# Batch 0 of an attention and MLP kernel begun in groups of 256 tokens, with q and k loaded by token

## The chip, the cores and the metric

The kernel runs on one core of a Trainium2 chip. A core has five engines that work side by side, each through its own list of instructions in strict order: TensorE (PE, matrix products; its weight loads are shown as PEld), VectorE (DVE), ScalarE (ACT), GpSimd (POOL) and SyncE (SP). DMA transfers can be issued by SP, ACT and POOL; those of SP and ACT are called hardware loads here, those of POOL software loads. The metric is device time in microseconds of one execution; the profile is of one execution.

## The reference

Attention over 4 batches of 8 heads, 768 tokens and head dimension 64, with a window of 128 tokens and 4 sink tokens that everyone sees, then a two-layer MLP with a squared relu on the 3072 rows that result:

```
scores = scale * np.matmul(q, k.transpose(0, 1, 3, 2))
keep = is_sink | in_window
scores = np.where(keep, scores, -1000000000.0)
a = np.exp(scores - max); a = a / (sum(a) + 1e-09)
x = np.matmul(a, v)            # heads side by side: 3072 x 512
g = np.maximum(x @ w_in, 0.0) ** 2     # 512 x 2048
out = g @ w_out                        # 2048 x 512
```

All inputs and the output are float32.

## The kernel before, in words

The batches are handled one after the other, overlapped. Within a batch the tokens are taken in blocks of 256 (three blocks, called s = 0, 1, 2 in the code) and the heads in four pairs (m = 0 to 3). For a pair and a block the steps are: q and k turned, so that the head dimension lies on the partitions (transposes on PE into a PSUM tile `pt`, then an "unload" that copies `pt` to `qkT`); scores on PE into `ps`; exponential on ACT into `expm`; a mask (DVE or POOL; in block 0 of batch 0 the mask is added by two matmuls of `sg`, so no mask step follows); values on PE into `po`; the division by the sum ("norm", a reciprocal and a product on DVE) into `xn_sb`; four transposes on PE into `px` and a copy to `xT`. Then layer 1 (`pm`, 16 matmuls for 4 of 16 column blocks and one block of tokens), relu (`r`), square (`gT_sb`) and layer 2 (`py`). For the sinks, `kblk` is filled by ACT from `qkT`, `pk` is a PE product with it, `es` its exponential on ACT, and `vs` a product on POOL that reads `vs_in`, a small load of the sink rows of v.

Batch 0 has the start to itself. Before the change its first two blocks come as one group of 512 tokens: eight loads of 256 KB, for k and q of each pair in turn, all issued by SP (line 351). Four tokens lie side by side on a partition, so each piece of memory read is 1 KB long. They arrive as fp32 in `qr`. A cast regroups them to bf16 (`qs`, line 194 on DVE, line 192 on ACT), PE turns four 128 x 128 tiles per load (line 507), and the unload puts tokens back in their order with a strided write. The third block comes later, loaded and cast by POOL (`qn`). Weights (`w_in_sb`, `w_out_sb`) and v are loaded and cast by POOL too.

What sets the order of all work is a list written out by hand in the file: `ORDER` names every step by its number, with a letter for the engine where there is a choice (`d` DVE, `a` ACT) and the PSUM pool behind a plus. The steps are recorded in that order, and each engine gets its instructions in it. `DUMMIES` gives, for some steps, a number of filler matmuls (line 185) that PE runs ahead of the step while it would otherwise wait. Line 1368 is a run of 29 such matmuls at the start. A hardware load signals its end on one of eight semaphores used in turn; a load that takes a semaphore again first waits for the load that had it before.

## Time and profile before

| | |
|---|---|
| median of three runs | 210.17 us (209.14 to 210.32) |
| span of the profiled execution | 208.6 us |
| what lies around the span, against the median | 1.6 us |
| PE busy in the span | 199.8 us, 96% |
| DVE, ACT, POOL busy | 86%, 64%, 47% |
| first layer-1 product on PE | at 17.13 us |

The profiled execution's own time is given as its span; the runs are timed without a profile. A row of the profile in order of time reads: start, length (both us), engine, line, operation, output and inputs, count, and in brackets how long the engine had been idle and what ended that. "PE 96%" is not a peak: fillers and waiting pipelines count as busy.

### The profile page before, as it was taken

To read this page: it belongs to the slowest core of one execution; us is meant where nothing else is said; L and a number is where in the kernel's file an instruction comes from. 1 tells how busy PE (TensorE), PEld (TensorE's weight loads), DVE (VectorE), ACT (ScalarE), POOL (GpSimd) and SP (SyncE) were. 2 spreads that over 40 slices of the span, in tenths; PEclk is the share of its full clock that TensorE was granted. 3 is DMA by queue.
4 is the path that set the end of the run, shared out by engine and by line. 5 is a ranking of instruction groups with operands and counts; after the bars stand their busy time and mean duration, and the time that the engine had idled before them with its cause. 6 is when DMAs were issued, how large, how long until landed. Compare 5 with 4: busy or idle time off the path is not lost.

```text
span 208.6 us, 6015 instructions
## 1 busy us (share of the span) xinstructions
PE 199.8 (96%) x2498; PEld 176.1 (84%) x2500; DVE 178.4 (86%) x342; ACT 133.0 (64%) x208; POOL 98.2 (47%) x138
## 2 busy tenths in 40 slices
PE   7789899999899999999999999999999999999993
PEld 7548796679778889989878988998889999999893
DVE  5757566996989998999998788999989998998853
ACT  2595728548988168899888448989871452584110
POOL 7988164999489936999423628000280000000000
PEclk9999999999999999999999999999999999999999
DMA  5999999999989999999998996901023220200205
GB/s 150 280 185 204 178 193 214 170 155 188 121 55 135 146 142 210 126 167 155 140 149 216 95 129 172 155 3 25 3 50 123 57 80 24 104 0 0 100 4 201
DMA packets 93994, 26.10 MB, mean 125 GB/s; under 512 B 86800, under 2 KB 91408, under 8 KB 93968
## 3 DMA queue, kind: packets, MB, share of 16 engines
q0 software_dynamic: 69248, 12.59, 79.6%
q1 hardware_dynamic: 24536, 13.01, 27.0%
q8 instruction: 19, 0.31, 0.6%
q10 hardware_dynamic: 184, 0.14, 0.2%
q14 instruction: 7, 0.06, 0.1%
HBM read 27.30 MB, written 6.29 MB: 161 GB/s over the span
## 4 chain that ended last, share of the span: by engine, by line
PE 65%; POOL 12%; DVE 9%; DMA 6%; ACT 3%; issue 2%; POOLq 0%; ACTq 0%
PE py L1238 25%; PE pm L891 25%; DMA w_in_sb<-in_moe_w_in_dram 6%; PE pm L763 4%; PE ps L613 4%; POOL v L381 3%; PE po L682 3%; POOL qn L372 3%; POOL vs L554 2%; PE py L1099 2%; ACT expm L634 1%; POOL expm L218 1%; PE pt L507 1%; DVE sg L1212 1%; POOL w_in_sb L308 1%
## 5 line engine op out<-in xcount | busy, mean ns | idle before, releaser
L634 ACT ACTIVATE expm<-ps 128x1024 bf16<-128x1024 f32 (+1 forms) x48 | 43.9, 951 | 9.4 <-PE ps L613 7.5
L218 POOL TENSOR_SCALAR_AFFINE_SELECT expm<-expm 128x512 bf16<-128x512 bf16 x34 | 25.4, 782 | 43.8 <-DVE xn_sb L699 19.5
L941 DVE CUSTOM_DVE_ANT_0 r<-pm,t 128x512 bf16<-128x512 f32 x54 | 36.1, 685 | 1.6 <-PE pm L891 1.1
L1238 PEld LDWEIGHTS <-gT_sb 128*128 128x128 bf16 x320 | 30.4, 98 | 4.5 <-issue 0.8
L891 PEld LDWEIGHTS <-w_in_sb 128*128 128x128 bf16 x384 | 32.4, 114 | 1.7 <-issue 1.5
L192 ACT ACTIVATE t<-pm 128x512 f32<-128x512 f32 x42 | 24.7, 600 | 13.5 <-PE pm L891 12.7
L891 PEld LDWEIGHTS <-wi 128*128 128x128 bf16 x288 | 24.7, 114 | 0.8 <-issue 0.7
L1238 PEld LDWEIGHTS <-sg 128*128 128x128 bf16 x240 | 22.4, 98 | 3.2 <-DVE sg L1212 0.3
L192 ACT ACTIVATE osb<-py 128x256 f32<-128x256 f32 (+1 forms) x36 | 14.1, 398 | 15.7 <-PE py L1238 15.0
L763 PE MATMUL pm<-xT,w_in_sb 128*128 128x256 bf16 x192 | 22.5, 273 | 1.0 <-DMA w_in_sb<-in_moe_w_in_dram 1.0
L763 PEld LDWEIGHTS <-w_in_sb 128*128 128x128 bf16 x192 | 20.5, 114 | 1.9 <-DMA w_in_sb<-in_moe_w_in_dram 1.2
L891 PE MATMUL pm<-xs,wi 128*128 128x256 bf16 (+1 forms) x192 | 21.6, 246 | 0.0
L891 PE MATMUL pm<-xs,w_in_sb 128*128 128x256 bf16 (+1 forms) x192 | 21.5, 246 | 0.0
L1238 PE MATMUL py<-wt,gT_sb 128*128 128x256 bf16 x160 | 20.7, 273 | 0.2
L1238 PE MATMUL py<-wt,sg 128*128 128x256 bf16 x160 | 20.8, 273 | 0.0
L1238 PE MATMUL py<-w_out_sb,gT_sb 128*128 128x256 bf16 x160 | 20.4, 273 | 0.0
L914 ACT ACTIVATE gT_sb<-r 128x1024 bf16<-128x1024 bf16 x17 | 18.0, 1056 | 1.8 <-DVE r L941 1.6
L682 PE MATMUL po<-v,expm 128*128 128x65 bf16 x352 | 17.9, 193 | 0.3 <-ACT expm L634 0.3
L682 PEld LDWEIGHTS <-expm 128*128 128x128 bf16 x352 | 16.7, 97 | 1.7 <-ACT expm L634 0.5
L699 DVE TENSOR_TENSOR xn_sb<-po,rc 128x512 bf16<-128x512 f32 (+1 forms) x28 | 17.2, 615 | 1.0
L1252 DVE TENSOR_TENSOR osb<-py,osb 128x256 f32<-128x256 f32 x30 | 12.1, 418 | 4.7 <-PE py L1238 4.6
L613 PE MATMUL ps<-qkT 64*128 64x128 bf16 (+1 forms) x256 | 14.3, 238 | 0.8 <-ACT expm L634 0.6
(109 smaller groups left out, 383.3 us busy)
## 6 DMA issues: line engine op xcount, KB each, us to landing
out_dram<-osb SPq DMA_DIRECT2D x11, 512.0 KB, 4.9
v<-in_v_dram POOLq DMA_DIRECT2D x24, 128.0 KB, 6.8
qn<-in_k_dram POOLq DMA_DIRECT2D x20, 128.0 KB, 6.5
qn<-in_q_dram POOLq DMA_DIRECT2D x20, 128.0 KB, 6.4
w_in_sb<-in_moe_w_in_dram POOLq DMA_DIRECT2D x4, 512.0 KB, 10.5
w_out_sb<-in_moe_w_out_dram POOLq DMA_DIRECT2D x4, 512.0 KB, 10.9
qr<-in_k_dram SPq DMA_DIRECT2D x4, 256.0 KB, 5.6
qr<-in_q_dram SPq DMA_DIRECT2D x4, 256.0 KB, 5.2
```

The costliest lines, as they stand in the source:

```text
L192: return nc.scalar.activation(out=dst, in_=src, func=AF.Copy)
L218: nc.gpsimd.affine_select(out=e_tile, in_=e_tile, compare_op=ALU.is_ge, fill=fill, base=i - 1, pattern=[[0, n], [1 if i else -1, 128]], ch ...
L613: nc.tensor.matmul(ps[:, h2, o:o + w], lhsT=qkT_sb[r, m, 1, c, :], rhs=qkT_sb[r, m, 0, qb:qb + w // 128, :], start=(i == 0 and not biased) ...
L634: nc.scalar.activation(out=x[:, :, o:512], in_=bank_t["s", b, s, m][:, :, o:512], func=AF.Exp, scale=scale)
L682: touch(("po", b, s, m0), e, nc.tensor.matmul(pv[:, i, h2, :], lhsT=lhsT, rhs=rhs, start=(n_ == 0), stop=(n_ == len(mms) - 1)), j)
L699: touch(("po", b, s, m0), e, nc.vector.tensor_tensor(out=xn_sb[:, 2 * s:2 * s + 2, 128 * (m0 + j0):128 * (m0 + j0 + nj)].rearrange("p i (j ...
L763: nc.tensor.matmul(pm[:, i, :], lhsT=w_in_sb[:, fb // 4, kb, fb % 4:512:4], rhs=xT[:, c0 // 256:(c0 + cw) // 256, kb, :], start=(kb == 0), ...
L891: touch(tag, e, nc.tensor.matmul(y[:, bk, i, :], lhsT=weights(name, f0 + i, a), rhs=rhs[:, a, :], start=fresh and i == 0 and a == 0, stop= ...
L914: nc.scalar.activation(out=d, in_=x, func=AF.Square)
L941: touch(tag, e, nc.vector._custom_dve(TENSOR_ADD_SAT, out=d.rearrange("p n c -> p (n c)"), in0=T["y"][:, 1].rearrange("p n c -> p (n c)"), ...
L1238: touch((b, u), e, nc.tensor.matmul(region(name), lhsT=x[:, i, :], rhs=w_[:, i, :], start=first and i == 0, stop=i == HB - 1, skip_group_c ...
L1252: ins = nc.vector.tensor_tensor(out=d, in0=region(of), in1=d, op=ALU.add)
```

## The change

- Batch 0 now comes in three groups of 256 tokens. The first two are loaded by 16 transfers of 128 KB, each for 128 tokens and four heads, one token per partition, so that each piece read is 256 bytes long. k is issued by SP, q by ACT, ahead of the small `vs_in` load that ACT issued first before.
- The casts are gone. PE turns the fp32 tiles themselves, against an fp32 copy of the identity (`ident32`, made by one DVE copy), eight tiles for two head pairs at a time, into fp32 PSUM. The unload casts to bf16 and writes without a stride.
- The first 180 or so steps of `ORDER` stand in another order, and the fillers in `DUMMIES` are placed anew (31 behind the start before, 46 now). From the third block of batch 0 on the list is the old one with new numbers.

```diff
 ORDER = """
-986 0 1 2 7 8 9 10 11 12 13 14 15 16 17 18 987+0 3 5 19 20 21 6 79 22 23 24 25 55d 56d 57+0 58 59 60a 83+0 85 103+1
...
+975 0 1 8 9 10 11 12 13 14 15 16 17 18 19 976+0 3 7 5 20 21 22 6 4 23 24 25 62 2 56+0 57d 58a 64+1 66 65+1 59+0 67 60d
...
 DUMMIES = {
-    987: 29, 58: 8, 63: 10, 64: 4, 83: 3, 91: 3, 97: 3,
+    976: 29, 59: 8, 72: 6, 85: 6, 76: 4, 88: 6, 80: 4, 103: 6, 145: 6,
 }
...
     def fill_one(i):
+        nc.vector.memset(v_sb[i][:, :, :, D:D + 1], 1.0)
         nc.vector.memset(kblk[i], 0.0)
         nc.vector.memset(vs_sb[i], 0.0)
-        nc.vector.memset(v_sb[i][:, :, :, D:D + 1], 1.0)
...
+    def build_ident32(e):
+        nc.vector.tensor_copy(out=ident32, in_=ident)
...
-    GROUPS[0] = [(0, 4), (512, 2)]
+    GROUPS[0] = [(0, 2), (256, 2), (512, 2)]
...
+    def load_qk(g, half, ti):
+        if not half:
+            qr_slot[ti, g] = Slot("qr", 2)
+        h0 = NP * half
         def run(e):
+            if not half:
+                qr_t[ti, g] = bank(qr_slot[ti, g], "qr", [128, 2, DM], FP32)
+            return [(nc.scalar, nc.sync)[ti].dma_start(
+                out=qr_t[ti, g][:, t, D * h0:D * h0 + D * NP].rearrange("p (h d) -> p h d", d=D),
+                in_=(q, k)[ti][0, h0:h0 + NP, 256 * g + 128 * t:256 * g + 128 * t + 128, :].rearrange("h p d -> p h d"))
+                for t in range(2)]
+        o = dma_op(("act", "sp")[ti], ("qk", 0, half, ti, g), run, 1.0, None, () if half else [qr_slot[ti, g]])
...
-                    def regroup(e, m=m, ti=ti):
-                        t = qs_t[b, m, ti, g] = bank(qs_slot[b, m, ti, g], "qs", [128, w, n, 2, D], BF16)
-                            copy(e, t[:, 0], qr_t[b, m, ti, g].rearrange("p h (t d) -> p t h d", d=D))
...
-                            bank_t[b, m, g] = bank(bs, "pt", [128, 2, 1024], BF16)
+                            bank_t[b, m, g] = bank(bs, "pt", [128, 2, 1024] if casted else [128, 2, 512],
+                                                   BF16 if casted else FP32)
...
-                                        if casted else qs[ti][:, j, t, :, :], rhs=ident, is_transpose=True,
+                                        if casted else qr_t[ti, g][:, t, 128 * (m + j):128 * (m + j) + 128],
+                                        rhs=ident if casted else ident32, is_transpose=True,
...
-    load_sinks("act", 0)
-    for m in range(NP):
-        for ti in (1, 0):
-            load_qk(0, m, ti, 0, 1)
+    for g in range(2):
+        for half in range(2):
+            for ti in (1, 0):
+                load_qk(g, half, ti)
+    load_sinks("act", 0)
```

ACT's list at the start, before, with the semaphores that each instruction waits for (DMAHW0 to DMAHW7 are those of hardware loads; `qkT<-pt` is an unload, `expm<-ps` an exponential, `qs<-qr` a cast):

```order
L424 DMA vs_in<-in_v_dram 32x1x64
L192 ACT_TABLE_LOAD
L192 ACTIVATE qkT_179<-pt 128x512 [waits PE_49]
L634 ACTIVATE expm<-ps 128x2x384 [waits PE_49]
L634 ACTIVATE expm<-ps 128x1024 [waits PE_49]
L192 ACTIVATE qkT_179<-pt 128x512 [waits PE_49] x2
L192 ACTIVATE qs<-qr 128x512 [waits DMAHW7_49,DVE_49]
L192 ACTIVATE qs<-qr 128x512 [waits DMAHW0_49,DVE_49]
L634 ACTIVATE expm<-ps 128x2x384 [waits PE_49]
```

The same place now:

```order
L346 DMA qr<-in_q_dram 128x4x64 x4
L346 DMA qr<-in_q_dram 128x4x64 [waits DMAHW0_49]
L346 DMA qr<-in_q_dram 128x4x64 [waits DMAHW2_49]
L346 DMA qr<-in_q_dram 128x4x64 [waits DMAHW4_49]
L346 DMA qr<-in_q_dram 128x4x64 [waits DMAHW6_49]
L418 DMA vs_in<-in_v_dram 32x1x64 [waits DMAHW0_49]
L193 ACT_TABLE_LOAD
L193 ACTIVATE qkT_180<-pt 128x2x256 [waits PE_49]
L599 ACTIVATE expm<-ps 128x2x384 [waits PE_49] x4
L599 ACTIVATE expm<-ps 128x1024 [waits PE_49] x4
```

Eight loads, of which five behind the first four (vs_in counted) wait for earlier loads, have moved ahead of ACT's table load, and ACT keeps one unload of eight.

DVE's list at the start, before, from its last memsets on (`xn_sb` is the norm):

```order
L233 MEMSET kblk_173 128x272
L234 MEMSET vs_175 128x520
L235 MEMSET v_182 128x48
L194 CAST qs<-qr 128x512 x2
L194 COPY qkT_179<-pt 128x512
L194 CAST qs<-qr 128x512 x4
L194 COPY qkT_179<-pt 128x512 x3
L698 RECIPROCAL rc<-po 128x4
L699 TENSOR_TENSOR xn_sb<-po,rc 128x2x128
```

The same place now:

```order
L195 CAST qkT_180<-pt 128x2x256 x3
L663 RECIPROCAL rc<-po 128x4
L664 TENSOR_TENSOR xn_sb<-po,rc 128x2x128
L663 RECIPROCAL rc<-po 128x4
L664 TENSOR_TENSOR xn_sb<-po,rc 128x2x128
L195 CAST qkT_180<-pt 128x2x256 x2
L663 RECIPROCAL rc<-po 128x4
L664 TENSOR_TENSOR xn_sb<-po,rc 128x2x128
L663 RECIPROCAL rc<-po 128x4
L664 TENSOR_TENSOR xn_sb<-po,rc 128x2x128
L195 CAST qkT_180<-pt 128x2x256 x2
```

The casts of loaded tiles are gone, seven unloads stand on DVE, and those of the second group are placed between the norms of the first block.

PE's list behind the 29 matmuls of the start, now (`pt<-ident,qr` is a transpose of a loaded tile, `ps<-sg,ident` the mask, `ps<-qkT` scores; LDWEIGHTS loads the weights of the matmul behind it):

```order
L482 MATMUL pt<-ident_166,qr 128x128 [waits DMAHW1_49,DVE_49]
L482 MATMUL pt<-ident_166,qr 128x128 [waits DMAHW3_49]
L482 MATMUL pt<-ident_166,qr 128x128 [waits DMAHW0_49]
L482 MATMUL pt<-ident_166,qr 128x128 [waits DMAHW2_49]
L482 MATMUL pt<-ident_166,qr 128x128 x4
L571 LDWEIGHTS ident [waits Pool_49]
L571 MATMUL ps<-sg,ident 128x384 [waits Pool_49]
L571 LDWEIGHTS ident
L571 MATMUL ps<-sg,ident 128x384
L578 LDWEIGHTS qkT_180 [waits Activation_49]
```

The same place before:

```order
L507 LDWEIGHTS qs [waits DVE_49]
L507 MATMUL pt<-ident,qs 128x128 [waits Pool_49]
L507 LDWEIGHTS qs
L507 MATMUL pt<-ident,qs 128x128
```

The transposes wait for loads instead of casts, eight stand together, and the first scores wait for an unload on ACT.

In layer 1, all eight products of the first two blocks now stand ahead of the third block's transposes and scores; before, one stood behind these transposes and one behind the third block's scores.

145 lines of the change are left out of this document (51 added, 94 removed).

## The prediction

> **What bounds the kernel now.** I read the page first, then busy time by stretch, then the order of time over the first 55 us, because the old and the new order of instructions agree behind that.
>
> ```profile
> span 208.6 us, 6015 instructions
> PE 199.8 (96%) x2498; PEld 176.1 (84%) x2500; DVE 178.4 (86%) x342; ACT 133.0 (64%) x208; POOL 98.2 (47%) x138
> ```
>
> ```profile
> 0.00:16.00 16.00, 12.72 (x162) 9.80 (x162) 10.16 (x29) 9.69 (x16) 13.37 (x27) 1.00 1.20 204
> 16.00:24.00 8.00, 7.96 (x116) 7.37 (x114) 6.31 (x15) 4.36 (x6) 5.26 (x7) 1.00 1.36 201
> 24.00:28.00 4.00, 3.00 (x32) 2.83 (x31) 2.37 (x4) 2.00 (x3) 1.34 (x3) 1.00 2.39 159
> 28.00:40.00 12.00, 11.95 (x118) 9.28 (x117) 8.43 (x11) 7.88 (x10) 8.06 (x9) 1.00 1.31 202
> 40.00:60.00 20.00, 19.37 (x236) 16.22 (x235) 17.28 (x29) 14.85 (x21) 15.93 (x22) 1.00 1.92 134
> 60.00:200.00 140.00, 139.59 (x1794) 125.96 (x1793) 129.08 (x246) 94.17 (x155) 54.20 (x73) 1.00 0.91 103
> ```
>
> The columns are PE, weight loads, DVE, ACT, POOL, clock, DMA share, GB/s. From 16 to 200 us PE is idle for 2.1 us out of 184. So PE carries everything behind the start, and the time is "when the dense part begins" plus a fixed amount of PE work plus few gaps. The change touches the part ahead of it. These rows, in order of time, carry that part:
>
> ```profile
> 0.82 0.46 SPq L351 DMA_DIRECT2D qr<-in_k_dram  x1
> 0.82 1.30 ACTq L424 DMA_DIRECT2D vs_in<-in_v_dram  x1
> 1.27 3.01 PEld L1368 LDWEIGHTS <-tri 128*128 128x128 bf16 x29 [1.27 <-DVE tri L224]
> 2.15 1.28 ACT L192 ACT_TABLE_LOAD   x1 [2.15 <-issue]
> 3.57 0.45 DVE L194 CAST qs<-qr 128x512 bf16<-128x512 f32 x1
> 4.50 0.47 SPq L351 DMA_DIRECT2D qr<-in_q_dram  x1
> 5.78 0.62 DVE L194 CAST qs<-qr 128x512 bf16<-128x512 f32 x1 [1.75 <-DMA qr<-in_q_dram]
> 6.89 0.60 ACT L192 ACTIVATE qkT<-pt 128x512 bf16<-128x512 bf16 x1 [3.45 <-PE pt L507]
> 7.50 2.35 DVE L194 CAST qs<-qr 128x512 bf16<-128x512 f32 x4 [0.51 <-DMA qr<-in_q_dram]
> 8.03 0.56 PEld L185 LDWEIGHTS <-ident 128*128 128x128 bf16 x10 [0.16 <-issue]
> 10.13 0.49 PE L606 MATMUL ps<-sg,ident 128*128 128x384 bf16 x2
> 10.67 0.34 PE L613 MATMUL ps<-qkT 64*128 64x256 bf16 x4
> 11.29 0.63 ACT L192 ACTIVATE qs<-qr 128x512 bf16<-128x512 f32 x1 [0.16 <-DMA qr<-in_q_dram]
> 13.29 0.35 PE L682 MATMUL po<-v,expm 128*128 128x65 bf16 x6
> 13.68 0.18 DVE L698 RECIPROCAL rc<-po 128x4 f32<-128x4 f32 x1 [0.58 <-PE po L682]
> 13.89 0.43 ACT L192 ACTIVATE kblk<-qkT 64x16 bf16<-64x16 bf16 x2
> 13.90 0.42 DVE L699 TENSOR_TENSOR xn_sb<-po,rc 128x256 bf16<-128x256 f32 x1
> 14.34 3.71 ACT L634 ACTIVATE expm<-ps 128x768 bf16<-128x768 f32 x4
> 16.91 0.29 PE L572 MATMUL pk<-qkT,kblk 128*32 128x256 bf16 x4
> 17.13 1.94 PE L763 MATMUL pm<-xT,w_in_sb 128*128 128x256 bf16 x16
> 25.55 5.43 PE L763 MATMUL pm<-xT,w_in_sb 128*128 128x256 bf16 x48 [1.00 <-DMA w_in_sb<-in_moe_w_in_dram]
> 30.82 1.06 PE L507 MATMUL pt<-ident,qn 128*128 128x128 bf16 x16
> 39.42 1.04 PE L989 MATMUL py<-w_out_sb,gT_sb 128*128 128x512 bf16 x4
> 53.63 0.40 PE L613 MATMUL ps<-qkT 64*128 64x128 bf16 x6 [0.58 <-ACT expm L634]
> ```
>
> The q and k loads become usable at 3.57 (first), 5.78 (second), 7.50 (fourth) and 11.3 (eighth, the last). From the last load a chain runs through cast, transpose, unload, scores, exponential, values and norm to the first layer-1 product at 17.13. There the dense part begins. It has two gaps: 1.00 us for the last w_in chunk, 0.58 us for an exponential.
>
> **The change part by part.** *Removed:* six casts on DVE and two on ACT (0.45 to 0.63 us each in the rows), about 4.7 us of work, part of it on the chain above. *Loads:* 2 MB as before, in 16 transfers of 128 KB instead of 8 of 256 KB, half of them issued by ACT. *Added wait:* hardware loads share eight semaphores. By the order, ACT issues four q loads, then its fifth waits for its first, and so on to the eighth. Then vs_in waits for the fifth q load, and the table load and every ACTIVATE stand behind it. In the old order ACT had one load ahead of the table load and was ready at 3.43.
>
> When is ACT free? The first issue on ACT took 1.30, three more at 0.47 end at 3.5. The fifth q load completes 1.25 MB of q and k. Between the fourth old load (1.0 MB at 7.50) and the eighth (2.0 MB at 11.3) that is about 8.4. Then vs_in has to be issued, for which SP's three give the length, and the table loads.
>
> ```profile
> L424 SPq DMA_DIRECT2D vs_in<-in_v_dram x3: 676/682/897, 5.0 to 6.8; - x3
> L507 PEld LDWEIGHTS <-qs x32: 96/98/151, 4.2 to 12.1; 128*128 128x128 bf16 x32
> L194 DVE COPY t<-pm 128x512 f32<-128x512 f32 x12 | 8.2, 687 | 1.0 <-ACT expm L634 0.6 <-PE pm L891 0.4
> ```
>
> 8.4 + 0.68 + 1.28 = 10.4. Bounds: 8.3, if the fifth lands 2.75 us after an issue at 3.6 as the first load did (0.82 to 3.57); 13.0, if it takes 6.8 us from an issue at 4.2 as the eighth did (4.50 to 11.3). I take 9.5, somewhat under the middle value, since q and k now have a queue each, and the queue rows below show that the engines can hold more than one transfer at a time (a share of 273%), while the one queue of the loads was at 95%.
>
> *The size of the pieces* (256 bytes instead of 1 KB) I cost at nothing. The first two rows (packets, MB written, share of the 16 engines) are of 4 to 8 us, when the q and k loads on SP's queue moved almost alone, the last of 44 to 50 us:
>
> ```profile
> q1 hardware_dynamic: 1149, 1.11, 94.8%
> q0 software_dynamic: 19, 0.00, 0.9%
> q0 software_dynamic: 6924, 0.87, 273.3%
> ```
>
> In the last row 6924 pieces, each read as 256 bytes, moved in 6 us, or 1154 per us; the 8192 new pieces would take 7.1 us, and the old loads spread over some 8. [...]
>
> *Transposes of fp32:* four batches of eight, with load and multiply in one instruction. Lower bound 8 x 0.066 = 0.5 us (the bf16 row at 30.82), upper 8 x 0.26 = 2.1 (a matmul of 512 columns, at 39.42). I take 8 x 0.098 = 0.8, one unoverlapped weight load each. *Unloads* that cast from fp32: between 0.45 (the fastest cast) and 0.69 (the f32 copy out of PSUM above); I take 0.65, near the row that also reads PSUM. Seven of the eight are now DVE's.
>
> Now the walk along the new order, which is strict on each engine. The first pair's scores wait for the one unload given to ACT, and behind them on PE wait all other transposes.
> - ACT unload 9.5 to 10.1. Two score groups on PE (0.34, then 0.49 whose tail overlaps, and 0.18): 10.8.
> - Eight fillers (0.056 each) and eight transposes with a tail of 0.16 (the 0.40 of four at 0.06): 12.2. Two unloads on DVE: 13.5.
> - Scores (0.2), values (0.2), scores of the last pair (0.5), six fillers: 14.8. Transposes of group 1: 15.7, values 16.0.
> - One norm (0.18 + 0.42; the order puts it ahead): 16.7. Two unloads: 18.0.
> - Scores (0.5), six fillers, transposes: 19.8. Two unloads: 21.1. Scores: 21.5.
> - Two exponentials (0.93 each, 3.71 / 4): 23.4. kblk: 23.8. Sink scores: 24.1, and layer 1 begins.
>
> That is 7.0 us later than 17.13. *Given back:* the 1.00 us wait for w_in goes, since six products that don't need the last chunk stand ahead of it; so do the 0.6 us at 53.63, since POOL and ACT are ahead by then. *Late next:* all eight layer-1 products now precede the third block's scores, so its four exponentials, two unloads, one relu and sink exponential (3.7 + 1.2 + 1.0 + 0.4 = 6.3 on ACT) meet only 5.5 us of PE work (transposes, scores, four py): 0.8 lost. *SP:* its last four k loads wait for its first four; behind them stand only the vs_in loads of later batches, which nobody needs before batch 1. *DVE:* the fp32 copy of the identity and the moved memsets end before the first load lands. *POOL:* its work on vs now waits for the later vs_in, and w_in chunks 2 and 3 are queued behind; I cost that at nothing, because the last chunk is needed some 10 us later than before. If it arrived after 36 us, the excess would count fully. The triangles moved ahead (0.5 us) are covered by the same.
>
> Sum: 7.0 - 1.0 - 0.6 + 0.8 = +6.2 us. The profiled execution has a span of 208.6; the runs' median of 210.17 lies 1.6 above it, which I take as what lies around the span. 208.6 + 6.2 + 1.6 = 216.4.
>
> **The rivals.**
> *Faster (the early start pays).* The last load no longer carries a cast and only half of the second block hangs on it: 10 (landing) + 1.0 (transposes) + 1.3 (unloads) + 0.4 + 1.9 + 0.4 + 0.3 = 15.3 for the first product, 1.8 before the old 17.13; with 1.0 of the w_in wait this gives 210.2 - 2.8 = 207.4. It needs ACT free by about 6.5 and the unloads of each pair hidden behind the pair before. Against it: the order's semaphores, and PE's order, in which each batch of transposes stands behind scores that wait for the last unloads.
> *Mostly hidden.* ACT free at 8.3, transposes at 0.5 (four batches), unloads at 0.45 (six on the chain): 1.2 + 1.2 + 1.2 off leaves +2.6, or 212.8; with one more pair of unloads overlapped (1.3), 211.5.
> [...]
> *PE slows down after its idle time.* From about 7.1 (first transposes and mask matmuls done) to 10.1 PE has nothing. The first weight loads of the kernel come 104 ns apart (3.01 / 29), those at 8.03 come 56 ns apart, so there is a slow pace at the start. If it came back, the 2.1 us of PE work that follow (scores 0.8, fillers 0.5, transposes 0.8) would double: 218.5. [...]
>
> **How the numbers follow.** The forecast (213 to 219) gets 0.62; faster 0.09; mostly hidden 0.09, nearly half of it within 0.5% of before; half pace 0.10; slow PE 0.10. About 0.5% (1.05 us) is what a measurement of this kernel can tell from no change. So faster 0.09, same 0.04, slower 0.87. The range 211.5 to 221.2 leaves out faster, the hidden case below it, and half of the half-pace case, 0.18 in all.
>
> **What would show it.** ACT's table load near 9 instead of 2.15 and its first unload near 10: the added wait. Gaps on PE ahead of the score matmuls, released by ACT first and DVE's unloads later; the first layer-1 product at 22 to 25. No wait for w_in afterwards. Fp32 transposes near 0.1 us each. Wrong if the table load comes before 6, or the first product before 19.

## The result, and the profile after

The changed kernel takes 225.46 us (median of four runs, 224.41 to 226.5), the kernel before 209.88 on the same occasion (four runs, 209.14 to 210.32): ratio 1.0742, 95% interval 1.0705 to 1.0779. That is 15.6 us slower; the forecast was 6.2 slower, 216.4, with 221.2 as the upper end. The profiled execution has a span of 224.3, 15.7 more than the 208.6 of before. (For one run below, half the loads with both edits, only the times are used: its profiled execution took 412.67 us, with its matmuls at about half pace (its first layer-1 product took 3.74 us, the run with kblk ahead has 1.94), for a reason the records don't show, and its other three took 215.7 to 216.0.)

The page of the changed kernel, first the span and the busy time, then the granted clock of PE in 40 slices:

```profile
span 224.3 us, 6045 instructions
PE 205.7 (92%) x2509; PEld 180.3 (80%) x2509; DVE 175.7 (78%) x341; ACT 130.4 (58%) x202; POOL 97.3 (43%) x138
...
PEclk9859969999999999999999999999999999999999
```

Busy time by stretch, in the stretches and columns shown for before (PE, weight loads, DVE, ACT, POOL, clock, DMA share, GB/s):

```profile
0.00:16.00 16.00, 8.93 (x63) 6.93 (x64) 3.19 (x13) 3.50 (x4) 8.30 (x19) 0.80 1.23 179
16.00:24.00 8.00, 5.93 (x86) 4.60 (x85) 4.73 (x12) 2.43 (x3) 5.71 (x9) 0.97 1.29 167
24.00:28.00 4.00, 2.42 (x37) 1.89 (x35) 2.55 (x5) 2.18 (x4) 3.65 (x5) 1.00 1.59 189
28.00:40.00 12.00, 10.44 (x120) 9.52 (x121) 5.09 (x13) 5.14 (x8) 5.87 (x9) 0.86 1.52 198
40.00:60.00 20.00, 19.17 (x202) 14.04 (x201) 13.64 (x22) 10.70 (x14) 8.85 (x10) 1.00 0.95 74
60.00:200.00 140.00, 137.90 (x1806) 124.54 (x1805) 128.97 (x245) 99.65 (x160) 64.90 (x88) 1.00 1.15 112
```

From 16 to 200 us PE is now idle for 8.1 us, where it was 2.1, and its clock is below 1 in three stretches, where it was 1.00 in all. PE's busy sum grew by 5.9 us, although the work hardly changed (2509 matmuls, before 2498): a slow matmul counts as busy (the first layer-1 product with 3.04 us, before with 1.94). (The clock reads 1.00 also ahead of its first record, at 6.24 us here, although the start ran slowly: its 29 weight loads are 104 ns apart, as they were before, against 56 at 8.03 us before, where the clock is 1.00.)

The start in order of time (start, length, engine, line, what, count, idle time before and what ended it):

```profile
0.82 7.55 ACTq L346 DMA_DIRECT2D qr<-in_q_dram  x8
9.21 1.26 ACTq L418 DMA_DIRECT2D vs_in<-in_v_dram  x1
10.50 1.28 ACT L193 ACT_TABLE_LOAD   x1 [10.50 <-issue]
11.80 0.60 ACT L193 ACTIVATE qkT<-pt 128x512 bf16<-128x512 f32 x1
12.45 0.50 PE L578 MATMUL ps<-qkT 64*128 64x256 bf16 x4 [5.56 <-ACT qkT L193]
14.07 1.03 PE L186 MATMUL pt<-ident 128*128 128x128 bf16 x8
14.90 1.81 PE L482 MATMUL pt<-ident,qr 128*128 128x128 f32 x8
17.68 1.74 POOL L519 TENSOR_TENSOR vs<-vs_in,head_rows 32x130 bf16<-32x130 f32 x4 [7.97 <-DMA vs_in<-in_v_dram]
18.10 0.34 PE L578 MATMUL ps<-qkT 64*128 64x256 bf16 x4 [0.72 <-DVE qkT L195]
19.60 1.04 PE L482 MATMUL pt<-ident,qr 128*128 128x128 f32 x8
22.75 0.61 PE L578 MATMUL ps<-qkT 64*128 64x128 bf16 x12 [1.35 <-DVE qkT L195]
26.08 0.51 PE L186 MATMUL ps<-ident 128*128 128x128 bf16 x6 [0.71 <-DVE qkT L195]
26.95 1.94 ACT L599 ACTIVATE expm<-ps 128x1024 bf16<-128x1024 f32 x2 [1.82 <-PE ps L578]
28.78 0.43 ACT L193 ACTIVATE kblk<-qkT 64x16 bf16<-64x16 bf16 x2
29.26 0.29 PE L537 MATMUL pk<-qkT,kblk 128*32 128x256 bf16 x4 [2.12 <-ACT kblk L193]
29.48 3.04 PE L728 MATMUL pm<-xT,w_in_sb 128*128 128x256 bf16 x16
```

Three pieces make up the 15.7 us. The first unload on ACT, for which the first scores wait, comes at 11.80 instead of 6.89: 4.9. From there to the first layer-1 product it takes 17.7 us (to 29.48) instead of 10.2 (to 17.13): 7.4. Behind the first product it takes 194.8 us instead of 191.5: 3.3. Inside the second piece stand PE's waits for two casts in a row on DVE (0.72, 1.35, 0.71), a wait of 2.12 for `kblk`, and matmuls at half pace (the transposes at 14.90 take 1.81, the same eight at 19.60 take 1.04).

### The profile page after: what moved, and what is told of

Read it like the earlier page. It is cut to its first block, busy times and chain, and to the rows that moved or that the text cites. A ratio compares the mean times of both kernels' runs of the same rounds, so it can differ in the third digit from the quotient of the medians.

```text
span 224.3 us, 6045 instructions
## 1 busy us (share of the span) xinstructions
PE 205.7 (92%) x2509; PEld 180.3 (80%) x2509; DVE 175.7 (78%) x341; ACT 130.4 (58%) x202; POOL 97.3 (43%) x138
## 4 chain that ended last, share of the span: by engine, by line
PE 67%; DVE 13%; ACT 7%; DMA 5%; issue 3%; SPq 2%; POOL 1%; ACTq 1%
PE py L1203 22%; PE pm L856 21%; PE pm L728 9%; PE po L647 5%; DMA qr<-in_q_dram 4%; PE ps L578 4%; PE pt L482 2%; ACT expm L599 2%; DMA qkT<-qn 2%; DVE qkT L195 2%; PE py L1064 2%; DVE xn_sb L664 2%; ACT qkT L193 1%; DVE r L906 1%; DVE sg L1177 1%
## 5 line engine op out<-in xcount | busy, mean ns | idle before, releaser
L856 PEld LDWEIGHTS <-w_in_sb 128*128 128x128 bf16 x384 | 32.5, 114 | 1.7 <-issue 1.5
L728 PE MATMUL pm<-xT,w_in_sb 128*128 128x256 bf16 x192 | 23.4, 281 | 0.4 <-DVE xT L195 0.3
L193 ACT ACTIVATE osb<-py 128x256 f32<-128x256 f32 (+1 forms) x36 | 14.0, 397 | 15.6 <-PE py L1203 15.0
L728 PEld LDWEIGHTS <-w_in_sb 128*128 128x128 bf16 x192 | 21.0, 116 | 1.7 <-issue 0.9
L578 PE MATMUL ps<-qkT 64*128 64x128 bf16 (+1 forms) x256 | 14.8, 241 | 8.2 <-ACT qkT L193 5.6
L578 PEld LDWEIGHTS <-qkT 64*128 64x128 bf16 x256 | 8.4, 94 | 14.7 <-ACT qkT L193 5.9
L647 PE MATMUL po<-v,expm 128*128 128x65 bf16 x352 | 18.5, 195 | 0.8 <-POOL expm L219 0.8
L647 PEld LDWEIGHTS <-expm 128*128 128x128 bf16 x352 | 17.4, 99 | 2.1 <-POOL expm L219 1.3
```

What stands on the lines that cost most here:

```text
L193: return nc.scalar.activation(out=dst, in_=src, func=AF.Copy)
L578: nc.tensor.matmul(ps[:, h2, o:o + w], lhsT=qkT_sb[r, m, 1, c, :], rhs=qkT_sb[r, m, 0, qb:qb + w // 128, :], start=(i == 0 and not biased) ...
L647: touch(("po", b, s, m0), e, nc.tensor.matmul(pv[:, i, h2, :], lhsT=lhsT, rhs=rhs, start=(n_ == 0), stop=(n_ == len(mms) - 1)), j)
L728: nc.tensor.matmul(pm[:, i, :], lhsT=w_in_sb[:, fb // 4, kb, fb % 4:512:4], rhs=xT[:, c0 // 256:(c0 + cw) // 256, kb, :], start=(kb == 0), ...
L856: touch(tag, e, nc.tensor.matmul(y[:, bk, i, :], lhsT=weights(name, f0 + i, a), rhs=rhs[:, a, :], start=fresh and i == 0 and a == 0, stop= ...
```

## The experiments

The theory of the prediction was that ACT's waits for semaphores delay the first unload and that the new order's own chain does the rest. Its rivals were late loads (small pieces), PE's clock, and POOL's hold-up, which the prediction had costed at nothing. "First unload" is the first on ACT, "first product" the first of layer 1 on PE; both are read from each run's order of time; a time is the median. The kernel before, run beside each, took 209.6 to 210.3.

| run | time, us | ratio to before (95%) | first unload | first product | span |
|---|---|---|---|---|---|
| changed kernel | 225.46 | 1.0742 (1.0705 to 1.0779) | 11.80 | 29.48 | 224.3 |
| q loads on SP too | 232.55 | 1.1056 (1.0986 to 1.1125) | 6.23 | 35.80 | 231.8 |
| vs_in first on ACT | 226.15 | 1.0753 (1.0699 to 1.0807) | 12.36 | 29.53 | 224.1 |
| more fillers | 224.1 | 1.0677 (1.0609 to 1.0744) | 12.55 | 30.56 | 223.1 |
| eight loads | 223.42 | 1.0646 (1.0585 to 1.0706) | 9.88 | 27.86 | 221.7 |
| q on SP, 512-byte pieces | 221.53 | 1.0540 (1.0486 to 1.0594) | 5.44 | 24.02 | 220.2 |
| half the loads | 220.97 | 1.0545 (1.0522 to 1.0569) | 7.43 | 24.84 | 218.2 |
| before, without casts | 209.82 | 1.0025 (0.9992 to 1.0059) | 6.23 | 16.75 | 208.1 |
| before, two queues | 212.79 | 1.0143 (1.0098 to 1.0187) | 9.58 | 20.90 | 211.3 |
| kblk ahead | 221.47 | 1.0542 (1.0496 to 1.0587) | 11.82 | 27.61 | 220.7 |
| kblk ahead, unloads split | 219.8 | 1.0473 (1.0419 to 1.0526) | 11.76 | 24.83 | 217.0 |
| eight loads, both edits | 219.3 | 1.0437 (1.0397 to 1.0478) | 9.78 | 23.62 | 217.6 |
| changed, 512-byte pieces | 224.81 | 1.0706 (1.0654 to 1.0758) | 10.62 | 28.09 | 221.9 |
| half the loads, both edits | 215.91 | 1.0300 (1.0271 to 1.0329) | | | |
| the same, PE kept busy | 212.86 | 1.0183 (1.0134 to 1.0233) | 7.35 | 18.85 | 210.9 |
| eight loads, both edits, PE kept busy | 219.07 | 1.0437 (1.0405 to 1.0468) | 10.63 | 24.38 | 216.5 |

### ACT freed: all q and k loads on SP

```diff
-            return [(nc.scalar, nc.sync)[ti].dma_start(
+            return [nc.sync.dma_start(
...
-        o = dma_op(("act", "sp")[ti], ("qk", 0, half, ti, g), run, 1.0, None, () if half else [qr_slot[ti, g]])
+        o = dma_op("sp", ("qk", 0, half, ti, g), run, 1.0, None, () if half else [qr_slot[ti, g]])
...
+    load_sinks("act", 0)
     for g in range(2):
...
-    load_sinks("act", 0)
```

> The changed kernel with all sixteen q and k loads issued by SP, and the first vs_in as ACT's only load, ahead of the table load. The waits for reused semaphores now stand on SP, where nothing urgent is behind them. Theory of the issuing engine (ACT's queue held the table load to 10.50 and the first unload to 11.80): table load near 2.2, first unload within 0.5 us of the end of the first transposes (6 to 8), no idle stretch of 5.6 us on PE, vs on POOL near 7 and w_in chunks 2 and 3 issued near 11; first layer-1 product 4 to 5 us earlier than 29.48, and the time 219 to 221. Theory of the order (the chain of transposes, unloads and scores is that long whenever it starts): first unload early as well, but the gaps only move behind it, time over 223. If the second group's loads land later from one queue, the gap returns ahead of the transposes at 14.9 or 19.6.

Both theories missed: 232.55, 7 us more than the changed kernel. ACT was indeed free (table load at 2.14, first unload at 6.23) and POOL's `vs` came at 9.72, but the second group's loads became the bound. PE's rows of this run:

```profile
17.16 1.33 PE L482 MATMUL pt<-ident,qr 128*128 128x128 f32 x5 [0.85 <-DMA qr<-in_q_dram]
...
25.95 0.48 PE L482 MATMUL pt<-ident,qr 128*128 128x128 f32 x1 [2.82 <-DMA qr<-in_q_dram]
29.20 1.33 PE L482 MATMUL pt<-ident,qr 128*128 128x128 f32 x5 [2.77 <-DMA qr<-in_q_dram]
```

What the DMA engines moved in it between 20 and 24 us, by queue (packets, MB, share of 16 engines; q1 carries SP's loads, q0 POOL's):

```profile
q0 software_dynamic: 631, 0.63, 92.0%
q1 hardware_dynamic: 632, 0.16, 30.0%
```

Equal numbers of packets, but a quarter of the bytes: beside `w_in` in 1 KB packets, the queue with 256-byte packets got a quarter of what the other got. That gave the next experiment. In the changed kernel no transpose but one at the start (0.24 us) waited for a load, since ACT's wait (5.56 us of PE) held them back.

### The size of the pieces, at the place where it showed

Same as the run above, but each piece takes two neighbouring tokens of a head. The transposes take the columns as they lie, so the scores of batch 0 are of the wrong pairs; the work is the same.

```diff
-                out=qr_t[ti, g][:, t, D * h0:D * h0 + D * NP].rearrange("p (h d) -> p h d", d=D),
-                in_=(q, k)[ti][0, h0:h0 + NP, 256 * g + 128 * t:256 * g + 128 * t + 128, :].rearrange("h p d -> p h d"))
-                for t in range(2)]
+                out=qr_t[ti, g].rearrange("p a b -> p (a b)").rearrange("p (h x) -> p h x", h=H)[:, h:h + 2, :],
+                in_=(q, k)[ti][0, h:h + 2, 256 * g:256 * g + 256, :].rearrange("h (p t) d -> p h (t d)", t=2))
+                for h in (h0, h0 + 2)]
```

> As the run with all q and k loads on SP (span 231.8, last loads of the second group usable only at 25.95 and 29.20), but each piece read is 512 bytes (two neighbouring tokens of a head) instead of 256; sixteen loads of 128 KB and all instructions stay. The tokens and heads that a transpose turns are mixed up by this, so the scores of batch 0 are of the wrong pairs; the work is the same. Theory of turns by piece (in that run between 20 and 24 us the loads' queue moved 632 pieces, the software queue 631, so bytes go by the size of the pieces): the q and k loads get twice the bytes beside v and w_in, the last one is usable before 19, first layer-1 product 8 to 12 us earlier, span 220 to 223. Rival (one queue, or SP's waits for semaphores, is what makes them late): the last load is still usable after 24, span over 228.

What the theory of turns by piece expected came: 221.53 instead of 232.55, span 220.2. The last wait of a transpose for a load ends at 14.63 instead of 29.20, and the first product comes at 24.02. The two queues between 12 and 16 us:

```profile
q1 hardware_dynamic: 1194, 0.57, 72.1%
q0 software_dynamic: 1187, 0.26, 69.8%
```

The same stretch of the run above, with pieces of 256 bytes:

```profile
q0 software_dynamic: 1396, 0.33, 84.6%
q1 hardware_dynamic: 1355, 0.34, 64.5%
```

In both the two queues' packet counts are nearly equal (1194 to 1187, 1355 to 1396), and q1 moves 0.57 MB instead of 0.34. The small pieces also take more of the engines' time for their bytes: 64.5% for 0.34 MB, against 72.1% for 0.57 MB, 1.5 times as much per MB. So two things are seen, a smaller share and a slower transfer. What came when little else moved is seen from 4 to 8 us, first before (1 KB pieces), then in the changed kernel (256 bytes, two queues), a fifth less:

```profile
DMA packets 1168, 1.11 MB, mean 279 GB/s; under 512 B 82, under 2 KB 1168, under 8 KB 1168
DMA packets 3581, 0.87 MB, mean 216 GB/s; under 512 B 3581, under 2 KB 3581, under 8 KB 3581
```

The same edit on the changed kernel as it is:

> The changed kernel as it is, q on ACT and k on SP in sixteen loads, but with 512-byte pieces (two neighbouring tokens of a head), so that the scores of batch 0 are of the wrong pairs and the work is the same. ACT's table load stands behind the q loads and vs_in here. If the size of the pieces sets when loads land beside the software queue: fifth to eighth q load and vs_in sooner, table load at 6.5 to 8.5 instead of 10.50, first unload 8 to 10 instead of 11.80, POOL's vs before 13 instead of 17.68, time 2 to 4 us less. Rival (pieces matter only on one queue, as in the run on SP): table load after 10, time within 1 us.

Neither: the table load comes at 9.33, between the two, the first unload 1.2 us earlier (10.62), the first product 1.4 (28.09). The time, 224.81, can't be told from 225.46 with these intervals. In the changed kernel the pieces thus cost about a microsecond at the start, not the 11 they cost on one queue.

### POOL's share: vs_in first on ACT

```diff
+    load_sinks("act", 0)
     for g in range(2):
         for half in range(2):
             for ti in (1, 0):
                 load_qk(g, half, ti)
-    load_sinks("act", 0)
```

> The changed kernel with the first vs_in issued by ACT ahead of its eight q loads instead of behind them; the table load still stands behind all eight. It parts POOL's share from ACT's. If the late vs_in (17.68 for POOL's work on vs, 19.37 for w_in chunks 2 and 3) costs time: vs near 7, chunks near 11, 1 to 2 us off, 223.5 to 224.5. If POOL's hold-up is hidden, as the prediction costed it: first unload still within 0.7 us of 11.80 (one more or one fewer issue ahead), first layer-1 product within 1 us of 29.48, time 224.5 to 226.

The rival held, with the time just above its range. POOL's `vs` came 8 us earlier (9.72 instead of 17.68) and w_in chunks 2 and 3 were issued at 11.46, but the first product stood at 29.53 and the time was 226.15. Behind the first product the profiled execution takes 194.6 us (changed kernel: 194.8). POOL's hold-up costs nothing that these runs can tell, as predicted.

### PE's clock: fillers in the gaps

```diff
-    976: 29, 59: 8, 72: 6, 85: 6, 76: 4, 88: 6, 80: 4, 103: 6, 145: 6,
+    976: 29, 64: 80, 59: 8, 72: 16, 85: 6, 76: 4, 93: 22, 88: 6, 80: 4, 103: 16, 91: 36, 145: 6,
```

> The changed kernel with 136 more filler matmuls on PE, put where it idles before about 28 us (80 ahead of the scores at 12.45, 10 each ahead of the scores at 18.10 and 26.52, 16 ahead of those at 22.75, 36 ahead of the sink scores at 29.26); nothing else moves. Theory of the slow clock (the idle stretch brings PE's clock down): granted clock 1.00 from 12 us on, the transposes at 14.90 take 1.04 instead of 1.81, the first layer-1 product 1.94 instead of 3.04, and 3 to 4 us come off: 221.5 to 222.5. Rival (PE's slow matmuls lie beside waits for ACT and DVE and only the product at 29.48 counts): 1 to 1.5 us off, 224. If the clock stays below 1 at 12 to 16 or 28 to 40 us, idling is not what lowers it.

Nearer the rival: 224.1, 1.4 us less. The fillers of the first gap and the mask's matmuls ended at 11.1, 2.1 us before the scores at 13.20, and the clock still fell, to 0.50 at 14.44. The first product took 1.94 at full clock but began at 30.56, since the fillers themselves delayed it, so that it ended at the same moment as before (32.5). This run does not settle what the slow clock costs; the run with PE kept busy, below, comes back to it.

### Fewer, larger loads

```diff
-                out=qr_t[ti, g][:, t, D * h0:D * h0 + D * NP].rearrange("p (h d) -> p h d", d=D),
-                in_=(q, k)[ti][0, h0:h0 + NP, 256 * g + 128 * t:256 * g + 128 * t + 128, :].rearrange("h p d -> p h d"))
-                for t in range(2)]
+                out=qr_t[ti, g][:, t, :].rearrange("p (h d) -> p h d", d=D),
+                in_=(q, k)[ti][0, :, 256 * g + 128 * t:256 * g + 128 * t + 128, :].rearrange("h p d -> p h d"))
+                for t in (half,)]
```

> The changed kernel with eight q and k loads of 256 KB (all heads of 128 tokens) instead of sixteen of 128 KB, still on two queues and with 256-byte pieces, and vs_in first on ACT. No load waits long for a semaphore, so ACT is free after five issues. Theory of the semaphore wait: table load at 4 to 5, first unload when the whole first group has landed and been turned (8 to 9), vs early; first layer-1 product 3 to 4 us earlier than 29.48, time 220 to 222.5. Rival (the pieces of 256 bytes or the two queues themselves are slow): the last load still lands after 14, the transposes of the second group wait for it, time over 223.

Half of it came: the table load at 7.21, the first unload at 9.88, which now waits for PE's transposes and these for the loads (the last wait for a load ends at 9.36); first product 1.6 us earlier, time 223.42. From the first unload to the first product it still takes 18.0 us, though it starts 1.9 us earlier. So the order was taken by itself.

### The order by itself: the second group's loads left out

The kernel leaves out the loads of queries and keys 256 to 511 of batch 0, 1 MB: the second group's transposes turn the first group's tokens again. `vs_in` goes first on ACT.

```diff
-                for t in range(2)]
+                for t in range(2 if g == 0 else 0)]
...
-                                        if casted else qr_t[ti, g][:, t, 128 * (m + j):128 * (m + j) + 128],
+                                        if casted else qr_t[ti, 0][:, t, 128 * (m + j):128 * (m + j) + 128],
```

> The changed kernel without the eight loads of the second group: its transposes turn the first group's tokens again (so queries and keys 256 to 511 of batch 0 are wrong), and vs_in goes first on ACT. No load waits for a semaphore on ACT, and nothing but the first group is waited for: what is left is the new order itself. From the run with eight loads (first unload 9.88, first layer-1 product 27.86) the chain between the two takes 18.0 us however early it starts. Theory of the order: first unload at 7 to 8, first product still 15 to 17.5 us behind it, at 23 to 25, against 10.2 us (6.89 to 17.13) before; span 217 to 219.5, so that 9 to 11 of the 15.7 us remain with no load in the way. Rival (late loads and ACT's waits are the loss): first product by 19, span under 213.

The theory of the order holds: first unload 7.43, first product 24.84, 17.4 us behind it; the profiled execution has a span of 218.2, 9.6 more than before. It was one of the two fastest of six; by the medians (220.97 against 209.59) 11.4 us remain, and late loads and ACT's waits are some 4.5 of the 15.6. The first group's loads are still waited for: two waits of PE, 0.78 and 0.88 us, end at 5.86 and 7.06.

### The parts of the change alone, on the kernel before

Without the casts, with the old loads, queue and order (columns that lie side by side are turned, so the scores of the first 512 tokens are of the wrong pairs):

```diff
-                            copy(e, t[:, 0], qr_t[b, m, ti, g].rearrange("p h (t d) -> p t h d", d=D))
+                        pass
...
-                                        if casted else qs[ti][:, j, t, :, :], rhs=ident, is_transpose=True,
+                                        if casted else qr_t[b, m, ti, g].rearrange("p a b -> p (a b)")[:, 128 * t:128 * t + 128], rhs=ident if casted else ident32, is_transpose=True,
```

> The kernel before with its own loads (1 KB pieces, one queue) and its own order, but without the eight casts of q and k: PE turns the fp32 loads with an fp32 identity and the unloads cast. Of a load, 128 columns that lie next to each other are turned, so the scores of the first 512 tokens of batch 0 are of the wrong pairs; the work is the same. It prices that part alone. If it pays: 0.45 to 0.6 us off the chain from each load to its transposes, the transposes 0.07 longer each (four in a row 0.3), unloads 0.65: first layer-1 product 16.3 to 17.1, time 0 to 1 us less than before. If PE pays for it: 16 transposes at 0.13 to 0.2 instead of 0.06, product 0.5 to 1 us later, time 0 to 1 us more.

The first product comes at 16.75, 0.4 us earlier, inside the first expectation; the time is the same (1.0025, 0.9992 to 1.0059). So leaving out the casts and turning fp32 tiles instead costs and gains nothing that can be told, and the 0.4 us of the start are not seen at the end.

The second queue alone:

```diff
-            return [nc.sync.dma_start(
+            return [(nc.scalar, nc.sync)[ti].dma_start(
...
-        o = dma_op("sp", ("qk", b, m0, ti, g), run, 16 * pairs * ROW[256 * n] + (0.7 if (b, m0, ti, g) == (0, 0, 0, 0) else 0.0), behind,
+        o = dma_op(("act", "sp")[ti], ("qk", b, m0, ti, g), run, 16 * pairs * ROW[256 * n] + (0.7 if (b, m0, ti, g) == (0, 0, 0, 0) else 0.0), behind,
```

> The kernel before with its four q loads issued by ACT behind vs_in instead of by SP, nothing else. Each queue has four loads and no issue waits long. It prices the second queue alone. ACT's table load goes from 2.15 to 4.3 to 5, still ahead of the first unload at 6.89. If two queues bring q and k sooner: the second load usable at 5.0 instead of 5.78, the last unchanged near 11, time 0 to 1 us less. If they only share the same engines: first load later by 0.3 to 0.7, time within 0.5 us.

Both missed: 212.79, 1.4% slower. The second queue brought no more data, 1.01 MB from 4 to 8 us against 1.11 before (all queues together), and the loads came in another order. DVE's cast of the first q load:

```profile
8.45 0.43 DVE L194 CAST qs<-qr 128x512 bf16<-128x512 f32 x1 [4.29 <-DMA qr<-in_q_dram]
```

It had stood at 5.78. The first q load is issued at 2.14, behind `vs_in`, while SP issues its four k loads from 0.82 to 2.91; three of these nobody needs yet. With the 128 KB loads of 512-byte pieces it is otherwise: over the first 8 us 196 GB/s came with two queues (the last run of the section on pieces) and 156 with one. PE, idle from 5.5 to 8.9, shows a granted clock of 0.57 from 8 to 16 us.

### The order's two costs: kblk and unloads in series

```diff
-61d 72+0 74 68+1 73+0 75 85+1 70 69 71 86d 87d 76+0 78 93+1 95 26 27 28 29 94+1 97 88+0 77 79 89d 90d 80+0 82 81d 83
-103+0 105 104+1 107 63 30 96 91+1 92 145+0 98d 106d 108d 146a 31 99+1 100 101 102 32 109+1 110 111 112 33 151+0 113+1
+61d 72+0 74 68+1 73+0 75 63 85+1 70 69 71 86d 87d 76+0 78 93+1 95 26 27 28 29 94+1 97 88+0 77 79 89d 90d 80+0 82 81d 83
+103+0 105 104+1 107 30 96 91+1 92 145+0 98d 106d 108d 146a 31 99+1 100 101 102 32 109+1 110 111 112 33 151+0 113+1
```

> The changed kernel with one step moved on ACT: the two copies into kblk, which need nothing of the second block, stand ahead of the second block's four exponentials instead of behind them. PE waits 2.12 us for kblk ahead of 29.26, and its clock is below 1 in the 3 us behind. If that wait is the order's own cost: the wait goes, sink scores stand right behind the scores of 26.52, first layer-1 product at 27.2 to 27.6 and at full clock (1.94 instead of 3.04), time 2 to 3.2 us less, 222.3 to 223.5. Rival: the work behind is bound by the second block's exponentials and the wait comes back at its values (32.32): 0 to 1 us less.

It holds, and more: 221.47, 4 us less; the sink scores follow at once and the first product runs at full clock.

```profile
27.39 0.29 PE L537 MATMUL pk<-qkT,kblk 128*32 128x256 bf16 x4
27.61 1.94 PE L728 MATMUL pm<-xT,w_in_sb 128*128 128x256 bf16 x16
```

The second edit, on top of the first:

```diff
-61d 72+0 74 68+1 73+0 75 63 85+1 70 69 71 86d 87d 76+0 78 93+1 95 26 27 28 29 94+1 97 88+0 77 79 89d 90d 80+0 82 81d 83
+61a 72+0 74 68+1 73+0 75 63 85+1 70 69 71 86d 87a 76+0 78 93+1 95 26 27 28 29 94+1 97 88+0 77 79 89d 90a 80+0 82 81d 83
```

> As the run with kblk ahead, and of each later pair of unloads (three pairs) one goes to ACT instead of both to DVE. In the changed kernel PE waits 0.72, 1.35 and 0.71 us for the second of two casts of 0.68 on DVE. If the unloads in series are the order's cost: each of these waits falls by 0.5 to 0.7, first layer-1 product 1.5 to 2 us earlier than with kblk alone, time as much less. Rival: ACT's exponentials stand ahead of its unloads (1.70 and 1.94 long), so that a wait for ACT takes the place of that for DVE: within 0.5 us of the run with kblk alone.

The theory of unloads in series holds: PE's three waits for casts are gone (0.24 for a norm is left at 20.61), the first product comes at 24.83, 2.8 us earlier, the time is 219.8, 1.7 less. Of the 2.8 us some 0.3 are the clock, not the edit: up to the second group of scores the run with kblk alone was slow for a stretch longer (0.50 instead of 0.34 for four scores).

Both on the version with eight loads:

> Both of these edits on the kernel with eight loads of 256 KB and vs_in first (223.4 us, first unload 9.88, first product 27.86). It is the best version of the new scheme that the runs so far point to. If the gains add up: 223.4 - 1.7 (wait for kblk, with its slow clock up to 3) - 1.7 (unloads) = 218.7 to 220.2, still slower than before by 4 to 5%. If loads become the bound once the order is shorter: a wait for the second group's loads (last one usable near 13) appears ahead of the second transposes and it stays over 221.

219.3, in the expected range, 4.1 us less than with eight loads alone.

### All causes at once

With half the loads left out as above, plus both edits:

> The run with half the loads (the second group's eight loads left out, its transposes turn the first group's tokens; span 218.2, first unload 7.43, first product 24.84) with kblk ahead of the second block's exponentials and the three later pairs of unloads split between DVE and ACT. If the causes add up: 24.84 - 2.1 (kblk) - 1.9 (unloads) = 20.6 to 21.2 for the first product, span 212.5 to 214. If a further price of the order shows: a new wait takes the place of these and the first product stays over 22, span over 215.

The time is 215.91, 5.1 us less than with half the loads alone. The spans of its runs, 213.9 to 214.3, lie at the upper end of what was expected if the causes add up (212.5 to 214), or just above it. Then 37 more matmuls at the start:

```diff
-    976: 29, 59: 8, 72: 6, 85: 6, 76: 4, 88: 6, 80: 4, 103: 6, 145: 6,
+    976: 66, 59: 8, 72: 6, 85: 6, 76: 4, 88: 6, 80: 4, 103: 6, 145: 6,
```

> As the run before it, with 37 more filler matmuls in the warm-up, so that PE is busy until about 6.5 instead of idling between its first transposes; the first unload may come up to 0.5 us later. If idling at 4.5 to 7 is what lowers the clock from 8.4 to 12 (mask matmuls 0.82 instead of 0.49, transposes 1.70 instead of 1.04): clock 1.00 there, first product 1 to 1.5 us earlier, 19.4 to 20, span 211 to 212.5, so that 2.5 to 4 us over the 208.6 of before remain for the order itself. Rival: the low clock comes from the fp32 transposes, whatever the idle time: no gain.

The time agrees with the clock theory: 212.86, 3.1 us less. Its busy time by stretch, the second transposes and the first product:

```profile
4.00:8.00 4.00, 4.00 (x53) 3.67 (x50) 0.21 (x1) 1.88 (x2) 3.71 (x8) 1.00 1.59 218
8.00:12.00 4.00, 4.00 (x49) 2.56 (x50) 1.39 (x4) 2.65 (x4) 3.82 (x8) 1.00 1.56 177
```

```profile
9.44 1.04 PE L482 MATMUL pt<-ident,qr 128*128 128x128 f32 x8
18.85 1.94 PE L728 MATMUL pm<-xT,w_in_sb 128*128 128x256 bf16 x16
```

From the first unload to the first product it takes 11.5 us. With both edits and a slow clock there (the run with unloads split) it takes 13.1, the same eight transposes 1.60 instead of 1.04. So about 1.6 of the 3.1 us is what faster matmuls would give; where the rest lies is not shown, since of the run without the added matmuls only times are used. That fp32 transposes lower the clock by themselves is ruled out here: all 32 are run, and the clock is 1.00 from 4 to 20 us.

So the times step down from 225.5 to 221.0 (the second group's loads left out), 215.9 (kblk ahead, unloads split), 212.9 (PE kept busy), against 209.7 for the kernel before: 4.5, 5.1, 3.1 in this order of removal, and 3.2 that remain. By the spans (210.9 against 208.6) 1.7 of what remains lies ahead of the first product and 0.6 behind it; what makes it up is not shown. Can a version that computes everything have this? The one with eight loads and both edits, with more matmuls at the start:

```diff
-    976: 29, 59: 8, 72: 6, 85: 6, 76: 4, 88: 6, 80: 4, 103: 6, 145: 6,
+    976: 108, 59: 8, 72: 6, 85: 6, 76: 4, 88: 6, 80: 4, 103: 6, 145: 6,
```

> The version with eight loads, kblk ahead and split unloads (219.3 us; first unload 9.78, first product 23.62, granted clock 0.57 from 8 to 16), with 79 more filler matmuls in the warm-up, so that PE is busy until its first group of q and k has landed at about 9.3. It computes the reference. If idle time ahead of the first transposes lowers the clock: clock 1.00 from 8 to 16, first unload at 9.5 to 10.2, first product 1.5 to 2.2 us earlier, 217 to 218 us, still 3.5 to 4% over the kernel before. If the late loads hide the slow clock: first product after 23, time over 218.5.

This one does not: the time stays at 219.07. In the profiled execution the clock is 1.00 up to 180 us, but the first product comes at 24.38, because the second group's transposes wait for a q load:

```profile
18.39 0.77 PE L482 MATMUL pt<-ident,qr 128*128 128x128 f32 x5 [2.04 <-DMA qr<-in_q_dram]
```

Without the added matmuls these transposes ran at 17.35 with no wait for a load. So PE is ready earlier (15.85), and the loads land later than in that run, the first group's too (its last wait ends at 10.26 instead of 9.26). Why they land later is not shown.

Of the versions that compute everything none comes nearer than 4% to the kernel before.

## Why the prediction was wrong

The direction was right, and so was the mechanism named first (ACT's table load behind waits for semaphores). The size was not: 6.2 us forecast, 15.7 by the spans. Three steps failed: the slow clock was left out of the sum (some 3.5 us by the rows), ACT's free time was put at 9.5 (11.80), and the stretch behind the first product was to become 0.8 us shorter (3.3 longer). Of the signs given, the table load (near 9) came at 10.50 and the first product (22 to 25) at 29.48. Term by term:

- *ACT free at 9.5.* It was 11.80: 2.3 us too low. 0.9 of it is the choice of 9.5 below the middle value of 10.4. The rest is in that value: `vs_in` was issued at 9.21, not 8.4, and its issue took 1.26, for which 0.68 had been taken from SP's later ones, though the row of the first issue on ACT (1.30) stood in the same profile. The argument for a value below the middle, that two queues hold more transfers at a time, has the run with two queues alone against it: there the first q load came 2.7 us later, 0.8 of it by being issued later (2.14 instead of 1.34).
- *The walk along the order.* From the first unload on it was right in kind and, in its later half, in size: two unloads 1.3 (forecast 1.3), the next group's transposes 1.05 (0.9), the last exponentials and kblk 2.3 (2.3). It failed at its second and third station, two score groups 1.7 instead of 0.7 and fillers with transposes 2.6 instead of 1.4: 2.2 us. With PE kept busy the two stations take 2.5 together (8.01 to 10.48), against 4.3 here and 2.1 in the forecast, so 1.8 of the 2.2 are slow clock and 0.4 the forecast's prices. Another 0.8 are fillers and transposes of 0.13 instead of 0.098 spread over the rest. The largest avoidable pieces of the walk, kblk behind the exponentials and both unloads on DVE, were in its 7.0 us without being named as avoidable; together they are worth 4.1 to 5.7 us (with eight loads, and on the changed kernel).
- *Given back 1.0 and 0.6, late next 0.8.* Forecast 0.8 less behind the first product, measured 3.3 more. The w_in wait did go. The wait for an exponential stayed (0.61 at 68.23), a wait of 0.83 for POOL's mask came at 54.66, and the first product and what follows ran at half clock for 3.4 us, which is 1.7 us of work. In all PE is busy 2.2 us longer behind the first product than before and idle 1.2 us longer, although the w_in wait is gone.
- *PE slows after idle time* was a rival with 0.10 and a price of 2.1 us. It came true together with the forecast's mechanism, in two places instead of one, and should not have been an alternative to it: the forecast itself said that PE would idle from 7.1 to 10.1. This is the step that cost most, some 3.5 us (1.8 in the walk, 1.7 behind it): half clock from 9.65 to 16.48 and from 30.13 to 33.54.
- *Loads at half the pace* (small pieces) was the other rival with 0.10, and 221.2, the upper end of the range, is its time. No run shows half the pace; what came from 4 to 8 us was a fifth less, 0.87 MB against 1.11. The size of the pieces does cost where the loads are the bound, 11.0 us between the two runs on one queue, and there the share beside a queue with larger packets is smaller too (0.16 MB against 0.63). The prediction's row of 1154 pieces per us came from a stretch without such a rival, which is why it said nothing of the share. In the changed kernel, where ACT's wait hides most of it, about 1 us.
- *Hidden costs that were hidden:* POOL (226.15 with `vs_in` early), and casts against fp32 transposes (same time). An unload took 0.60 on ACT and 0.69 on DVE (forecast 0.65).

2.3 for ACT, 2.2 for the second and third station of the walk, 0.8 for the rest of it and 4.1 behind it make 9.4 of the 9.5 us that were missing.

## What to carry to other kernels

When a forecast contains a stretch in which PE has nothing to do, the slow clock belongs into its sum, not beside it as a rival: here the clock was 0.50 from 9.65, within PE's wait of 5.56 us, to 16.48, and from 30.13, behind the wait of 2.12, to 33.54, some 3.5 us in all. And fillers should reach to the end of the gap: 80 of them, which with the mask's matmuls ended 2.1 us before it, were followed by 0.50 from 14.44 to 17.85. Where transfers of different queues overlap, compare the size of their packets as well as their bytes: here the small ones lost in proportion (0.16 MB against 0.63 at 632 and 631 packets). Walk a new order engine by engine and ask at each wait whether the released work needed to stand there: two copies behind four exponentials cost 4.0 us here, the casts that the change removed nothing that could be told.

## What the runs showed of the hardware that was not expected

In the changed kernel's trace PE's clock changes at 9.65, 16.48, 30.13 and 33.54 us; these lie 6.83, 13.65 and 3.41 us apart, 2, 4 and 1 times 3.41. The kernel's busy time, cut at that length (columns as above; the second number is PE's busy time, the third from the end the clock):

```profile
6.24:9.65 3.41, 0.65 (x5) 0.25 (x3) 0.69 (x1) 0.00 (x0) 3.34 (x8) 1.00 1.72 196
9.65:13.06 3.41, 0.61 (x5) 0.26 (x6) 0.00 (x0) 1.94 (x3) 0.06 (x1) 0.50 1.41 195
13.06:16.48 3.42, 3.42 (x22) 2.54 (x21) 0.00 (x0) 1.56 (x2) 0.00 (x0) 0.50 1.41 196
16.48:19.89 3.41, 2.69 (x35) 1.66 (x34) 1.90 (x4) 1.33 (x2) 2.04 (x5) 1.00 1.65 188
19.89:23.30 3.41, 2.06 (x41) 1.76 (x40) 2.37 (x7) 0.39 (x2) 3.41 (x5) 1.00 0.90 134
23.30:26.72 3.42, 2.71 (x42) 2.41 (x40) 2.45 (x7) 1.83 (x2) 2.63 (x5) 1.00 1.24 206
26.72:30.13 3.41, 1.28 (x22) 0.94 (x17) 1.94 (x3) 2.62 (x5) 3.41 (x6) 1.00 2.39 154
30.13:33.54 3.41, 3.41 (x34) 2.78 (x33) 0.28 (x2) 0.98 (x1) 2.85 (x4) 0.50 1.82 195
```

In each of these rows the clock is 1.00 or 0.50. Of the rows at 1.00, those with 0.65 and 1.28 us of PE work are followed by one at 0.50, those with 2.06 to 2.71 by one at 1.00. The run with half the loads has a row between these:

```profile
4.88:8.30 3.42, 1.76 (x13) 0.95 (x12) 0.43 (x1) 1.27 (x2) 3.35 (x8) 1.00 1.80 205
8.30:11.72 3.42, 3.42 (x25) 2.44 (x22) 0.26 (x1) 1.62 (x2) 3.25 (x7) 0.50 1.50 187
```

1.76 us of work in 3.42, and the next row is at 0.50. (1.29 of the 1.76 are fp32 transposes, and no run shows whether these weigh like other matmuls; the row with 1.28 has none.) Of the changed kernel's rows at 0.50, the one with 0.61 us of work (from 9.65) is followed by another at 0.50, the one with 3.42 (from 13.06) by one at 1.00. By windows of half a microsecond the clock of the second queue alone is at 0.50 from 8.35 to 15.18, with PE's work beginning again at 8.94, and that of kblk ahead from 8.54 to 18.78, with work from 12.47 on. With more fillers PE's idle time of 2.08 us lies in a stretch (11.03 to 14.44) with 1.33 us of work, and the next one is at 0.50. From the end of PE's wait to the fall of the clock it took 0.87 us here (29.26 to 30.13) and 1.24 with more fillers (13.20 to 14.44); both times the clock stayed at 0.50 for 3.41 us. What makes the clock fall and rise is not shown beyond these rows.

The queues' packet counts were nearly equal in the stretches shown above, 631 to 632 with packets of 1 KB and 256 bytes, 1187 to 1194 with 0.26 and 0.57 MB, and so were those of three queues of the changed kernel from 12 to 16 us (833, 842 and 833). In other stretches the counts differ (1528 to 1175 from 8 to 12 us with all loads on SP); what sets them is not shown.
